# Storing converted weight units from ScalarE's queue, one step behind their conversion

## The chip, the cores and the metric

The kernel runs on one core of a Trainium2 chip. The metric is the device time of one execution in microseconds (us). The engines are named as the profile names them: PE (TensorE's matmuls) and PEld (its weight loads), DVE (VectorE), ACT (ScalarE), POOL (GpSimd) and SP (SyncE). SP computes nothing; it issues transfers.

## The reference

Three stages follow one another, all in float32.

1. A linear recurrence with a complex decay over 768 positions, for 2 x 8 heads of width 48: `S = a * S + k v^T`, `y = q S`. Its output is reshaped to `x` with 1536 rows of 384.
2. A mixture of 8 experts: each row goes to the expert with the largest of `x @ w_gate`, and becomes `gate_w * (relu(x @ w1[e]) @ w2[e])`, with `w1[e]` 384 x 1024 and `w2[e]` 1024 x 384.
3. A gated product: `out = ((x @ w_a) * (x @ w_b)) @ w_out`, with `w_a`, `w_b` 384 x 1536 and `w_out` 1536 x 384. These three arrive as 64-bit floating-point numbers, and the kernel itself turns them into 32-bit ones.

## The kernel before

The three stages run in this order; the change lies in the second, the expert stage, from about 235 to 380 us.

**The expert stage.** Each of the 8 experts is four steps `fp`, so there are 32 steps `i = 4 * e + fp`, written out in one loop (L1064). In a step, TensorE runs `hmm(i)` (18 products for 256 hidden columns, L1023, and ACT's and DVE's readout of them) and `ymm(i - 1)` (18 products of the second layer, L1039). A product in float32 is made of three: every operand is split into a high part (ACT) and a low part (DVE: value minus high part). So behind each `hmm` ACT writes `hh` (L1027) and DVE writes `hl` (L1028), and `ymm` reads both. In the step `fp = 1` TensorE also turns the rows of the next expert (`expert_x`, L1004), split by ACT and DVE into `XTT` (L1011, L1013). After the last `ymm` of an expert its sums are copied to `x2h` (ACT, L1042) and `x2l` (DVE, L1043). `bounds()` puts one tiny product `fp` (L986) into step 10.

**Weights of the next expert.** `wload(e + 1, 1)` at `fp = 0` and `wload(e + 2, 0)` at `fp = 2` load 1536 KB each on SP's queue (L717) into two buffers in turn; a load waits until the split of what the buffer held is done. `wsplit` splits a quarter of an expert's weights per step: ACT's cast (L730), then DVE's subtraction (L734).

**Units of the last stage's weights.** The first third of `w_a`, `w_b` and `w_out` is converted during the earlier stages, in 12 units of 384 KB (0 to 3 of `w_a`, 4 to 7 of `w_b`, 8 to 11 of `w_out`). A unit is loaded into a tile `raw` on SP's queue (`raw_load`, L746, L748), converted by five operations of DVE and one of ACT into a tile `cvt` (`conv_g`, L757 to L765), put on the list `pend`, and stored as 192 KB of float32 into a DRAM array `wf` (`store`, L774). Units 0 to 2 go this way in the first stage. The dictionary `UE` (L1047) says which unit is converted beside which expert: unit 3 beside expert 0, units 4 and 5 beside expert 1, 6 and 7 beside expert 2, then one per expert. Where there are two, the first is converted in step `fp = 2` and the second in `fp = 3`; where there is one, it takes both steps. `store()` is called at `fp = 0` of the next expert (L1089), on SP's queue, after that step's loads; for the last unit it is called at the start of step 28 (L1071).

`m2load(w)` reads `wf[w]` back in steps 26, 27 and 28 (L791), and `m2split` splits it (L795, L796): parts 0 and 1 in steps 28 and 29, part 2 after the last `ymm`.

**Buffers.** `hh`, `hl`, `raw`, `cvt` and the rows `R` of an expert are all tiles with the tag "T", for which there are nine buffers (L61, L62). A new tile takes over a buffer once all that reads or writes its last content is done; for a `cvt` tile that is its store.

**Order.** The order of the instructions of each engine is that of the program (L37, a manual schedule). Each engine takes its own instructions in order, and so does each queue of transfers: one that waits holds up those behind it on the same queue.

Of the kernel before, what the change touches and what calls it, by code (L numbers as in the profile page):

```python
# [35 lines left out]
def build(tc, *args, **kw):  # L36
    with tc.manual_schedule():  # L37
        body(tc, *args, **kw)


def body(tc, q, k, v, a_re, a_im, w_gate, w1, w2, cap, w_a, w_b, w_o, out, dbg=None):
    nc = tc.nc
# [9 lines left out]
    def tS(shape, dt, name):  # L52
        return mp.tile(shape, dt, tag="S", name=name, bufs=2)
# [7 lines left out]
    def tT(shape, dt, name):  # L61
        return mp.tile(shape, dt, tag="T", name=name, bufs=9)  # L62
# [325 lines left out]
    def run(g):  # L388
        for _ in g:
            pass  # L390
# [323 lines left out]
    def wload(e, w):  # L714
        WR[w, e] = tS([128, 2, 3 * FF // 2], F32, f"wr{w}_{e}")
        src = (w1, w2)[w][e]
        nc.sync.dma_start(WR[w, e].rearrange("p a r -> p (a r)").rearrange("p (k f) -> p k f", k=(KD, KF)[w]), src.rearrange("(k p) f -> p k f", p=128))  # L717

    def wsplit(e, part):
        run(wsplit_g(e, part, 1))  # L720
# [48 lines left out]
            return x.rearrange("p (k f) -> p k f", k=KD)[:, :, u * 128:(u + 1) * 128]  # L769
        return x[:, u * CU:(u + 1) * CU]  # L770

    def store():
        for dst, src in pend:
            nc.sync.dma_start(dst, src)  # L774
        pend.clear()

    def conv_out(w, u, t):
# [11 lines left out]
    def m2load(w):  # L789
        m2r[w] = tS([128, 1536], F32, f"m2r{w}")  # L790
        nc.sync.dma_start(m2r[w], wf[w])  # L791

    def m2split(w):
        hl, r = m2tile(w, 0), m2r[w]
        A.copy(hl[:, 0], r)  # L795
        V.tensor_tensor(hl[:, 1], r, hl[:, 0].bitcast(F32), ALU.subtract)  # L796
# [29 lines left out]
    for c in range(NC):  # L826
# [39 lines left out]
        if c < NU0:  # L866
            store()
            if c + 1 < NU0:
                conv_load(u0[c + 1][0], 0, u0[c + 1][1], cv[:, (c + 1) % 2, :2 * CU])
            x = cv[:, c % 2]  # L870
            conv_out(*u0[c], conv(u0[c][0], 0, u0[c][1], x[:, 2 * CU:3 * CU], x[:, 3 * CU:]))
        if c == 3:
            store()
            wload(0, 0)
            wload(0, 1)
# [4 lines left out]
    def raw_load(n):  # L880
        conv_load(u0[n][0], 0, u0[n][1], tT([128, 2 * CU], I32, f"raw{n}"))

    def conv_tt(n):
        x = tT([128, 2 * CU], I32, f"cvt{n}")
        yield from conv_g(u0[n][0], 0, u0[n][1], x[:, :CU], x[:, CU:])
        conv_out(*u0[n], x[:, CU:].bitcast(F32))
# [10 lines left out]
    def pse(shape, name, tag, bufs):  # L897
        return ep.tile(shape, F32, tag=tag, name=name, bufs=bufs)
# [96 lines left out]
    def load_x(e):  # L995
        R = Rt[e] = tT([SP, 2, DM], F32, f"R{e}")
        after(nc.sync.dma_start(R, xs[e * NT:e * NT + SLOT].rearrange("(a p) d -> p a d", p=SP)), xs_sc)

    def expert_x(e):
        R = Rt[e]  # L1000
        xp = [pse([128, KD, SP], f"xp{e}_{a}", f"xp{a}", 1) for a in range(2)]
        for a in range(2):
            for kk in range(KD):
                PE.transpose(xp[a][:, kk], R[:, a, kk * 128:(kk + 1) * 128], ident[:SP, :SP])  # L1004
        X = XT[e] = XTT[:, e % 2]

        def o(i):
            return X[:, i].rearrange("p k (a t) -> p k a t", a=2)

        for a in range(2):  # L1010
            A.copy(o(0)[:, :, a], xp[a])  # L1011
        for a in range(2):
            V.tensor_tensor(o(1)[:, :, a], xp[a], o(0)[:, :, a].bitcast(F32), ALU.subtract)  # L1013

    def hmm(e, fp):
        hp = pse([128, 2, SLOT], f"h{e}_{fp}", "h", 3)
        W = WHL[0, e]
        for f2 in range(2):
            f = fp * 2 + f2
            i = 0  # L1020
            for a, b in ((0, 0), (1, 0), (0, 1)):
                for kk in range(KD):
                    PE.matmul(hp[:, f2], W[:, a, kk, f * 128:(f + 1) * 128], XT[e][:, b, kk], start=(i == 0), stop=(i == 3 * KD - 1))  # L1023
                    i += 1
        hi = tT([128, 2, SLOT], F32R, f"hh{e}_{fp}")
        lo = tT([128, 2, SLOT], F32R, f"hl{e}_{fp}")
        A.activation(hi, hp, AF.Relu)  # L1027
        V.scalar_tensor_tensor(lo, hp, 0.0, hi.bitcast(F32), ALU.max, ALU.subtract)  # L1028
        Hp[e, fp] = hi, lo

    def ymm(e, fp):
        if fp == 0:
            yps[e] = [y[:, e % 2] for y in YPS]
        W = WHL[1, e]
        for d in range(KD):
            for f2 in range(2):
                f = fp * 2 + f2
                for i, (a, b) in enumerate(((0, 0), (0, 1), (1, 0))):
                    PE.matmul(yps[e][d], W[:, a, f, d * 128:(d + 1) * 128], Hp[e, fp][b][:, f2], start=(f == 0 and i == 0), stop=(f == KF - 1 and i == 2))  # L1039
            if fp == 3:  # L1040
                hi, lo = (x[:, ds(offs[e], SLOT)] for x in x2[d])
                A.copy(hi, yps[e][d])  # L1042
                V.tensor_tensor(lo, yps[e][d], hi.bitcast(F32), ALU.subtract)  # L1043
# [17 lines left out]
    def load_off(e):  # L1061
        offs[e] = nc.values_load(off_i[:, e:e + 1], engines=[mybir.EngineType.Activation, mybir.EngineType.DVE], min_val=0, max_val=NT, skip_runtime_bounds_check_because="exclusive prefix sums of counts that add up to NT")
    bd = bounds()
    for i, (e, fp) in enumerate(seq):  # L1064
        if fp == 0 and e + 1 < E:
            load_x(e + 1)
            wload(e + 1, 1)
        if fp == 2 and e + 2 < E:
            wload(e + 2, 0)
        if i == 28:  # L1070
            store()  # L1071
        if i >= 26 and i < 29:
            m2load(i - 26)
        hmm(e, fp)
        if i == 0:
            next(tb)
        if i == 6:
            run(tb)
        if fp == 2:
            load_off(e)  # L1080
        if i in (2, 4, 10, 11, 12):
            next(bd, None)
        if i > 0:
            ymm(*seq[i - 1])
        if fp == 1 and e + 1 < E:
            expert_x(e + 1)
        us = UE.get(e, ())
        if fp == 0 and us:
            store()  # L1089
        if fp < len(us) and e > 0:  # L1090
            raw_load(us[fp])
        if len(us) == 2 and fp > 1:
            run(conv_tt(us[fp - 2]))
        elif us and fp == 2:
            cg = conv_tt(us[0])
            next(cg)
            next(cg)
        elif us and fp == 3:
            run(cg)
        if e + 1 < E:  # L1100
            wsplit(e + 1, fp)
        elif fp < 2:
            m2split(fp)
# [257 lines left out]
```

## Time and profile before

| | us |
|---|---|
| three runs | 610.43, 617.68, 617.88 (median 617.68) |
| profiled execution | 616.19 |
| its span, first to last instruction | 614.5 |
| PE busy | 513.5 (84%) |
| DVE busy | 436.3 (71%) |
| ACT busy | 277.3 (45%) |
| mean granted clock of TensorE | 0.948 |

The busy shares are of the whole span. The granted clock is a share of full speed (2.4 GHz). An engine's idle time is listed with what ended it, the releaser.

### The profile page before, as it was taken

To read this page: it belongs to the slowest core of one execution; us is meant where nothing else is said; L and a number is where in the kernel's file an instruction comes from. 1 tells how busy PE (TensorE), PEld (TensorE's weight loads), DVE (VectorE), ACT (ScalarE), POOL (GpSimd) and SP (SyncE) were. 2 spreads that over 40 slices of the span, in tenths; PEclk is the share of its full clock that TensorE was granted. 3 is DMA by queue.
4 is the path that set the end of the run, shared out by engine and by line. 5 is a ranking of instruction groups with operands and counts; after the bars stand their busy time and mean duration, and the time that the engine had idled before them with its cause. 6 is when DMAs were issued, how large, how long until landed. Compare 5 with 4: busy or idle time off the path is not lost. (4 is left out here: it accounts for less than half of the span.)

```text
span 614.5 us, 10390 instructions
## 1 busy us (share of the span) xinstructions
PE 513.5 (84%) x4030; PEld 456.8 (74%) x4030; DVE 436.3 (71%) x957; ACT 277.3 (45%) x491; POOL 78.4 (13%) x127
## 2 busy tenths in 40 slices
PE   0064754799899878987999999999999999999993
PEld 0022322579889748987899999888888888888992
DVE  6899999974998964796687884766666767623331
ACT  6566563684344443643566563343443333211220
POOL 2000000040134273011221000000000000002121
PEclk9987687869999988998999999999999999999998
DMA  4248742298966127868587644121212121001010
GB/s 153 53 144 217 227 112 81 61 170 189 217 182 236 48 85 228 262 167 275 179 269 253 219 160 126 51 78 51 78 53 78 52 77 53 2 0 52 20 58 30
DMA packets 63249, 77.56 MB, mean 126 GB/s; under 512 B 29464, under 2 KB 53144, under 8 KB 63192
## 3 DMA queue, kind: packets, MB, share of 16 engines
q1 hardware_dynamic: 60208, 68.75, 38.6%
q0 software_dynamic: 2576, 7.68, 4.4%
q8 instruction: 33, 0.54, 0.4%
q10 hardware_dynamic: 408, 0.39, 0.2%
q14 instruction: 24, 0.20, 0.1%
HBM read 61.27 MB, written 15.54 MB: 125 GB/s over the span
## 5 line engine op out<-in xcount | busy, mean ns | idle before, releaser
L1126 PE MATMUL ab<-x2h,m2h 128*128 128x512 f32 (+1 forms) x480 | 142.1, 369 | 0.0
L1126 PEld LDWEIGHTS ab<-x2h,m2h 128*128 128x128 f32 x480 | 87.4, 188 | 14.4
L1126 PE MATMUL ab<-x2l,m2h 128*128 128x512 f32 (+1 forms) x240 | 88.8, 370 | 0.0
L319 PE MATMUL n<-temps,ident 128*128 128x384 f32 x40 | 28.0, 866 | 56.9 <-ACT temps L316 56.9
L1142 PE MATMUL o<-m2h,gh 128*128 128x384 f32 x288 | 73.6, 336 | 0.0
L1023 PE MATMUL h<-XTT,whl 128*128 128x240 f32 x576 | 71.8, 279 | 0.6 <-ACT XTT L1011 0.6
L1039 PE MATMUL yps<-hh,whl 128*128 128x240 f32 x384 | 71.7, 279 | 0.8 <-DVE x2l L1043 0.8
L1023 PEld LDWEIGHTS h<-XTT,whl 128*128 128x128 f32 x576 | 68.6, 193 | 0.9 <-ACT XTT L1011 0.9
L734 DVE TENSOR_TENSOR whl<-wr,whl 128x1536 fp32r<-128x1536 f32 (+1 forms) x38 | 57.1, 1502 | 12.8 <-ACT whl L730 12.7
L319 PEld LDWEIGHTS n<-temps,ident 128*128 128x128 f32 x40 | 12.0, 325 | 70.0 <-issue 37.2
L1039 PEld LDWEIGHTS yps<-hh,whl 128*128 128x128 f32 x384 | 61.7, 194 | 1.0 <-DVE x2l L1043 0.9
L1133 DVE TENSOR_TENSOR g<-ab,g 128x512 f32<-128x512 f32 (+1 forms) x40 | 25.5, 638 | 45.8 <-PE ab L1126 45.8
L1039 PE MATMUL yps<-hl,whl 128*128 128x240 f32 x192 | 53.9, 281 | 2.3 <-DVE hl L1028 2.3
L1142 PEld LDWEIGHTS o<-m2h,gh 128*128 128x128 f32 x288 | 52.5, 188 | 2.4
L1126 PEld LDWEIGHTS ab<-x2l,m2h 128*128 128x128 f32 x240 | 45.2, 188 | 6.9
L1142 PE MATMUL o<-m2h,gl 128*128 128x384 f32 x144 | 48.5, 337 | 0.0
L1134 ACT CAST gh<-g 128x512 fp32r<-128x512 f32 (+1 forms) x40 | 23.2, 580 | 56.1 <-DVE g L1133 52.7
L730 ACT CAST whl<-wr 128x1536 fp32r<-128x1536 f32 x32 | 47.4, 1480 | 0.0
L1135 DVE TENSOR_TENSOR gl<-g,gh 128x512 fp32r<-128x512 f32 (+1 forms) x40 | 25.6, 639 | 25.8 <-ACT gh L1134 25.3
L1160 POOL DMA_INDIRECT out_dram<-acc,MT x12 | 11.7, 974 | 251.0 <-DVE acc L1158 248.7
L1039 PEld LDWEIGHTS yps<-hl,whl 128*128 128x128 f32 x192 | 37.0, 193 | 2.7 <-DVE hl L1028 2.7
L1132 ACT COPY g<-ab 128x512 f32<-128x512 f32 (+1 forms) x40 | 21.6, 541 | 28.9 <-PE ab L1126 27.7
(233 smaller groups left out, 946.0 us busy)
## 6 DMA issues: line engine op xcount, KB each, us to landing
wr<-in_moe_w_dram SPq DMA_DIRECT2D x16, 1536.0 KB
kid<-KL SPq DMA_DIRECT2D x5, 896.0 KB
cv<-in_moe_w_a_dram SPq DMA_DIRECT2D x11, 384.0 KB
KN<-kid SPq DMA_DIRECT2D x5, 672.0 KB
cv<-in_moe_w_b_dram SPq DMA_DIRECT2D x8, 384.0 KB
cv<-in_moe_w_out_dram SPq DMA_DIRECT2D x8, 384.0 KB
xs<-zt POOLq DMA_DIRECT2D x1, 2880.0 KB, 17.9
R<-xs SPq DMA_DIRECT2D x8, 360.0 KB
```

The source lines that it names most:

```text
L319: PE.matmul(n2, ident, sq[:, :, c], start=(c == 0), stop=(c == 1))
L730: A.copy(hl[:, 0, sl], WR[w, e][:, hf])
L734: V.tensor_tensor(hl[:, 1, x], WR[w, e][:, hf, i * n:(i + 1) * n], hl[:, 0, x].bitcast(F32), ALU.subtract)
L1023: PE.matmul(hp[:, f2], W[:, a, kk, f * 128:(f + 1) * 128], XT[e][:, b, kk], start=(i == 0), stop=(i == 3 * KD - 1))
L1039: PE.matmul(yps[e][d], W[:, a, f, d * 128:(d + 1) * 128], Hp[e, fp][b][:, f2], start=(f == 0 and i == 0), stop=(f == KF - 1 and i == 2))
L1126: PE.matmul(p, W[:, a].rearrange("p (k f) -> p k f", k=KD)[:, kk, (f % 4) * 128:(f % 4 + 1) * 128], x2[kk][b][:, c0:c0 + n], start=(i == 0 ...
L1132: A.copy(g, ps[0])
L1133: V.tensor_tensor(g, ps[1], g, ALU.mult)
L1134: A.copy(gh, g)
L1135: V.tensor_tensor(gl, g, gh.bitcast(F32), ALU.subtract)
L1142: PE.matmul(ops[s4], g[a][:, s4 * 128:(s4 + 1) * 128], W[:, b, f % 4], start=(f % 4 == 0 and i == 0), stop=(f % 4 == 3 and i == 2))
L1160: d = G.indirect_dma_start(out=out, out_offset=bass.IndirectOffsetOnAxis(ap=MT[:, i, 0:1].bitcast(U32), axis=0), in_=acc, in_offset=None)
```

## The change

`store` gets the engine that issues it as an argument. In the expert stage it is called in every step, right behind `hmm` and so behind `hh` on ACT's queue, and the two calls on SP are taken out. `m2load(2)`, which reads what the store of unit 11 writes, moves behind the store in step 28. The calls of `store()` in the first stage stay on SP.

```diff
-    def store():
+    def store(eng=nc.sync):
         for dst, src in pend:
-            nc.sync.dma_start(dst, src)
+            eng.dma_start(dst, src)
         pend.clear()
...
-        if i == 28:
-            store()
-        if i >= 26 and i < 29:
+        if i >= 26 and i < 28:
             m2load(i - 26)
         hmm(e, fp)
+        store(nc.scalar)
+        if i == 28:
+            m2load(2)
...
         us = UE.get(e, ())
-        if fp == 0 and us:
-            store()
         if fp < len(us) and e > 0:
             raw_load(us[fp])
```

## Rows read from the trace of the kernel before

**Rows 1.** Busy us by engine (x instructions), then PEclk, DMA share, GB/s.
```profile
285.00:287.00 2.00, 2.00 (x11) 2.00 (x11) 2.00 (x3) 0.00 (x0) 1.11 (x1) 0.50 0.75 193
```

**Rows 2.** Waits from 235 to 385 us: engine, line, releaser, total us, times, longest.
```profile
DVE hl L1028 <- DMA wf<-cvt: 9.9, 2, 5.9
...
ACT hh L1027 <- DMA wf<-cvt: 5.0, 4, 1.8
...
PE fp L986 <- DVE XTT L1013: 4.4, 1, 4.4
...
PE yps L1039 <- DVE hl L1028: 2.3, 2, 1.5
...
PE yps L1039 <- DVE x2l L1043: 0.8, 1, 0.8
```

**Rows 3.** Timeline of PE: start us, us, instruction [idle before and releaser].
```profile
258.45 2.26 PE L1023 MATMUL h<-XTT,whl 128*128 128x240 f32 x18
...
262.58 2.18 PE L1023 MATMUL h<-XTT,whl 128*128 128x240 f32 x18
...
277.37 2.26 PE L1023 MATMUL h<-XTT,whl 128*128 128x240 f32 x18
284.01 0.19 PE L986 MATMUL fp<-ones_f,okm 128*1 128x1 f32 x2 [4.38 <-DVE XTT L1013]
...
287.88 2.18 PE L1023 MATMUL h<-XTT,whl 128*128 128x240 f32 x18
...
300.56 2.27 PE L1023 MATMUL h<-XTT,whl 128*128 128x240 f32 x18
...
306.44 2.19 PE L1023 MATMUL h<-XTT,whl 128*128 128x240 f32 x18
```

**Rows 4.** Timeline of DVE around the conversions of units 4 and 5.
```profile
266.88 0.56 DVE L765 SCALAR_TENSOR_TENSOR cvt<-raw,cvt 128x384 f32<-128x384 f32 x1
...
271.54 0.56 DVE L765 SCALAR_TENSOR_TENSOR cvt<-raw,cvt 128x384 f32<-128x384 f32 x1
...
273.68 0.65 DVE L1028 SCALAR_TENSOR_TENSOR hl<-h,hh 128x480 fp32r<-128x480 f32 x1
...
275.19 1.75 DVE L734 TENSOR_TENSOR whl<-wr,whl 128x1536 fp32r<-128x1536 f32 x1
282.86 0.66 DVE L1028 SCALAR_TENSOR_TENSOR hl<-h,hh 128x480 fp32r<-128x480 f32 x1 [5.92 <-DMA wf<-cvt]
```

**Rows 5.** Timeline of SP's queue: transfers as they are issued.
```profile
273.79 0.37 SPq L717 DMA_DIRECT2D wr<-in_moe_w_dram  x1
274.21 1.75 SPq L774 DMA_DIRECT2D wf<-cvt  x2
...
295.99 1.25 SPq L774 DMA_DIRECT2D wf<-cvt  x2
```

**Rows 6.** Timeline of ACT in steps 7 and 8.
```profile
267.23 0.59 ACT L1027 ACTIVATE hh<-h 128x480 fp32r<-128x480 f32 x1
270.01 0.58 ACT L760 ACTIVATE raw<-raw 128x384 f32<-128x384 f32 x1 [2.19 <-DVE cvt L757]
...
271.85 0.58 ACT L1027 ACTIVATE hh<-h 128x480 fp32r<-128x480 f32 x1
...
273.05 1.50 ACT L730 CAST whl<-wr 128x1536 fp32r<-128x1536 f32 x1
```

**Rows 7.** Issue of one transfer, ns min/median/max: on ACT's queue, the stores on SP's.
```profile
L416 ACTq DMA_DIRECT2D temps<-in_a_im_dram x3: 603/608/1213, 0.9 to 2.8; - x3
...
L774 SPq DMA_DIRECT2D wf<-cvt x9: 426/581/1617, 254.3 to 365.6; - x9
```

**Rows 8.** The last store, its reader, and ACT's split of what that loads.
```profile
365.64 0.43 SPq L774 DMA_DIRECT2D wf<-cvt  x1
370.34 0.32 SPq L791 DMA_DIRECT2D m2r<-wf  x1
...
379.51 1.48 ACT L795 CAST m2h<-m2r 128x1536 fp32r<-128x1536 f32 x1
```

## The prediction

> **What bounds the kernel now.** I first read the busy time of each engine in short stretches. In the expert stage TensorE is busy in nearly every microsecond, so only what TensorE itself waits for can be gained there. So the second view was the list of waits of this stage, from 235 to 385 us, read for TensorE alone: there are three matmul entries in all, 4.4, 2.3 and 0.8 us [rows 2]. Nothing else stops TensorE between 235 and 385 us.
>
> Next I asked what stands behind the 4.4. TensorE's program order is hmm(10), a tiny matmul `fp`, ymm(9), hmm(11). The timeline shows hmm(10) from 277.37 to 279.63 and then nothing until `fp` at 284.01 [rows 3]; `fp` needs a PSUM buffer that VectorE frees with its XTT subtraction, and VectorE does that right after the lo half of step 9, `hl`. VectorE finished its weight split at 276.94 and then stood still for 5.92 us until 282.86 [rows 4]. The releaser named is the transfer wf<-cvt. `hl` does not read wf or cvt. It writes a tile of tag "T", of which there are nine buffers, and the buffer it was given had held the converted unit 4. A buffer whose content is still being stored can't be overwritten. This is the mechanism on which everything else rests.
>
> Why is that store so late? The conversion of unit 4 ended at 266.88 + 0.56 = 267.44 [rows 4]. Its store left SP only at 274.21, in one piece of 1.75 us with unit 5's, right behind a 1536 KB weight load issued at 273.79 [rows 5], which itself waits for the weight split of step 7. So unit 4 lay ready for 6.8 us, and then its 192 KB queued behind 1536 KB: 282.86 - 274.21 = 8.65 us from issue to release.
>
> The same happens one expert later: units 6 and 7 leave at 295.99 [rows 5], step 13's `hl` waits 9.9 - 5.9 = 4.0 us for the transfer, and TensorE loses 1.5 us of the 2.3 [rows 2]. From expert 3 on there is one unit per expert. There it is ACT's `hh` that waits for the transfer, up to 1.8 us at a time [rows 2], and no TensorE entry answers to it: TensorE runs on.
>
> **The change part by part.** *Nine stores move from SP's queue to ACT's, behind hh of the next step.* For units 3, 5, 7, 8, 9, 10 and 11 that is the same step as before; only units 4 and 6 go one step earlier. But on SP a store also stood behind the load of the next expert's second weights; on ACT it does not.
>
> *Gain at the first place.* Unit 4: ACT's hh of step 7 ends at 267.23 + 0.59 = 267.82 [rows 6], the conversion is 0.4 us older, so the store is issued at 267.8 without waiting. Its landing is bounded from both sides by two stores of the trace: 4.7 us (unit 11, 365.64 until the load that waits for it at 370.34 [rows 8]) and 8.65 us. So it lands between 272.5 and 276.5, and VectorE could not start step 9's hl before 276.94 anyway. The stall goes entirely. What it costs now: from the start of hmm(10) to that of hmm(11) are 287.88 - 277.37 = 10.51 us; the same stretch one expert earlier, hmm(6) to hmm(7), took 262.58 - 258.45 = 4.13 [rows 3]. The difference, **6.38 us**, is more than the 4.4 us of waiting: after the idle time the granted clock is 0.50, the 1.2 GHz level [rows 1], and the matmuls of ymm(9) run at half speed. Without the idle time I count this back too.
>
> *Gain at the second place.* hmm(14) to hmm(15): 306.44 - 300.56 = 5.88 us, less 4.13: **1.75 us** [rows 3].
>
> *Gain in experts 3 to 6.* ACT's four waits for the transfer, 5.0 us together [rows 2], disappear; TensorE never waited for them, so 0.
>
> *What takes the stall's place.* VectorE is the next to be late: with two units per expert it is filled with conversions and splits, and its lag already shows as TensorE waits of 0.84 (in the 2.3) and 0.8 us in steps 7 and 8 [rows 2]. Those two lie before the removed stall and stay. With the 6 us of slip gone, steps 10 to 12 can show the same: VectorE works through unit 6, which must have been loaded in time behind the 1536 KB. Bounds: 0, and the two known lags together, 1.6 us. I take **0.4**, nearer 0, since steps 11 and 12, the other two with such a load, show no lag of this kind today, and raw loads no longer stand behind two stores.
>
> *Cost on ACT.* One DMA issue on ACT took 0.6 us (median of three); stores on SP took 0.43 to 1.62 us [rows 7]; below 0.43 there is nothing to gain. I take 0.6, since it is the only row of ACT. Behind the store of unit 4 ACT's next work starts at 270.01, 2.2 us later: hidden. Behind unit 5's store (hh of step 8 ends 272.43, conversion ends 272.10 [rows 4, 6], so no wait) stand three x2h copies, the weight cast and hh of step 9. The cast would end at 273.05 + 1.50 + 0.6 = 275.15, and VectorE takes it up at 275.19 [rows 4, 6]: just hidden. At 1.6 us VectorE would start 1 us later, and step 9's hl with it; ymm(9) needs hl only once TensorE has finished hmm(10), at 279.63, so that too is covered. In one-unit experts ACT has more room. Sum 0, up to 1 us.
>
> *Relief on SP.* SP loses nine issues of 0.6 us; loads behind them go out earlier by that. Nobody waits for SP's own time; 0.
>
> *The last load, m2load(2), moves behind the store of unit 11.* It reads what that store writes. The store left SP at 365.64, the load at 370.34, and its reader on ACT starts at 379.51, behind the last copies of the expert stage [rows 8]. On ACT the store goes out after hh of step 28, some 2 us earlier than on SP. Even if it were 4 us later the load (4.7 us) would land by 379.0. Cost 0.
>
> **Sum**, against the profiled execution's own 616.19 us (span 614.5 and 1.69 around it): 616.19 - 6.38 - 1.75 + 0.4 = 608.5. The profiled run lies 1.5 us under the median of the three runs shown (617.68; the lowest is 610.43), so the same sum on the median gives 609.9. I say **609**.
>
> **The rivals.** *(a) The queue makes no difference to the landing, and the buffer is asked for sooner.* The row: the store of unit 4 needed 8.65 us behind 1536 KB, and at 267.8 another weight load is still under way. The tile allocator hands buffers on in the order in which they come free; with the store a step earlier, unit 4's buffer may go to step 8's hl (273.68) rather than step 9's. If the store again takes 8.65 us, it lands at 276.5, and VectorE stands for 2.8 us in step 8 [rows 4], which has no slack (TensorE already waits there). At the second place I count the 1.75 us as lost again. The gain shrinks from 8.1 to 3.6: 612.6, on the median 614.1. For it: the transfer engines are shared, seen in the 8.65. Against: two things must come together. The Trainium skill, DMA: Bandwidth & Descriptors, section "Issuing engines are not separate DMA queues", speaks for it: transfers started by any engine run on the same 16 DMA engines, so issuing from another one saves only sequencer time. By that rule alone the queue gives nothing, and only the earlier issue counts. The same page, "Queues, rings and completion order", says that each DMA engine takes the queues it has work for in turn, packet by packet; by that a store on ACT's queue need not sit out the whole load. No row of the trace has both queues loaded at once.
>
> *(b) It doesn't do what it says.* The releaser at 282.86 is inferred. If what really landed then were the weight load that was in flight ahead of the store, the stall would stay: 616 to 618. Against: hl reads no loaded tile, and the same releaser stands at both places.
>
> *(c) Slower.* An issue on ACT blocks everything behind it. If each of the nine takes over 0.9 us out of TensorE's path, the 8.1 us are spent; at SP's longest 1.62 us each, none hidden, 9 x 1.6 = 14.6 against 8.1: 622.7. The place would be the three x2h copies behind each store at an expert's start. Against: ACT's own issues took 0.6 us [rows 7], and at the tightest place that is just hidden.
>
> *(d) More than the sum.* The three runs differ by 7 us. If the lowest, 610.43, still holds the two stalls, the changed kernel would show 603 to 604. More likely the low run is one in which the store happened to land early.
>
> **How the numbers follow.** Forecast 0.68, (a) 0.16, (b) 0.06, (c) 0.04, (d) 0.06. The likeliest case's own range is 606 to 611.5 (1.6 us of VectorE lag and 1 us of ACT above, no lag and the profiled base below). The range for 8 in 10 goes from 604.5 to 614.5, which takes in (a) and leaves out (b), (c) and most of (d). Two per cent, about what a measurement of this kernel can tell from no change, is 12.4 us: under 605.3 lie most of (d) and a tail of the forecast, 0.09; over 630 only a worse form of (c), 0.02; the rest, 0.89, is within 2%.
>
> **What would show it.** Right: no wait of hl for wf<-cvt; hmm(10) to hmm(11) about 4.2 us; no stretch of granted clock 0.50 after it; ACT issues of about 0.6 us at some 0.1 us after hh. Wrong: a wait of hl or hh for wf<-cvt in steps 8 or 12 (a); the wait at step 9 unchanged, now put down to a load (b); x2h or the weight cast late behind a store, with TensorE waiting for x2l (c); VectorE waiting for a raw load in step 10, by more than 1.6 us.

## The result, and the profile after

The changed kernel takes 608.36 us (median of four runs, 605.37 to 609.29) against 617.3 for the kernel before. The ratio is 0.987, with a 95% interval of 0.982 to 0.992. A second measurement, `again` below, gave 608.81 against 619.19, ratio 0.983 (0.979 to 0.987). The forecast was 609.

Four entries of the list of waits of the changed kernel, from 230 to 375 us (engine, line, releaser, total us, times, longest):

```profile
DVE hl L1028 <- ACT hh L1027: 7.0, 2, 3.9
...
PE yps L1039 <- DVE x2l L1043: 1.6, 2, 0.8
DVE cvt L757 <- DMA raw<-in_moe_w_b_dram: 1.4, 1, 1.4
...
PE yps L1039 <- DVE hl L1028: 0.8, 1, 0.8
```

In this list hl waits for ACT's hh alone; the entries of hl and of hh for wf<-cvt [rows 2] are gone, and so is the wait of `fp`, 4.4 us. Two entries are new in size: TensorE's wait for x2l has doubled, and VectorE waits for a raw load.

The timeline of PE in the changed kernel, to be read beside [rows 3] (hmm of steps 6, 7, 10, 11, 13, 14, 15):

```profile
254.11 2.26 PE L1023 MATMUL h<-XTT,whl 128*128 128x240 f32 x18
258.24 2.18 PE L1023 MATMUL h<-XTT,whl 128*128 128x240 f32 x18
...
273.00 2.26 PE L1023 MATMUL h<-XTT,whl 128*128 128x240 f32 x18
277.44 2.18 PE L1023 MATMUL h<-XTT,whl 128*128 128x240 f32 x18
...
285.71 2.19 PE L1023 MATMUL h<-XTT,whl 128*128 128x240 f32 x18
288.74 0.38 PE L1039 MATMUL yps<-hh,whl 128*128 128x240 f32 x1 [0.84 <-DVE x2l L1043]
291.41 2.26 PE L1023 MATMUL h<-XTT,whl 128*128 128x240 f32 x18
295.54 2.18 PE L1023 MATMUL h<-XTT,whl 128*128 128x240 f32 x18
```

Step 10 falls from 10.51 to 4.44 us and step 14 from 5.88 to 4.13. Step 13 grows from 4.60 to 5.70. The two-microsecond stretches show no slow clock behind step 10; the one with the end of the changed kernel's ymm(9) and the start of hmm(11) reads (columns as in [rows 1]):

```profile
276.00:278.00 2.00, 2.00 (x20) 2.00 (x19) 1.53 (x2) 0.00 (x0) 0.92 (x1) 1.00 1.09 365
```

where the clock column (third from the end) shows 1.00; in before it read 0.50 during ymm(9) [rows 1].

What VectorE and ACT do in steps 7 to 10 now. First ACT with its queue, then VectorE (beside [rows 4, 6]):

```profile
262.89 0.57 ACT L1027 ACTIVATE hh<-h 128x480 fp32r<-128x480 f32 x1
263.12 0.54 ACTq L774 DMA_DIRECT2D wf<-cvt  x1
265.64 0.57 ACT L760 ACTIVATE raw<-raw 128x384 f32<-128x384 f32 x1 [2.19 <-DVE cvt L757]
...
267.49 0.55 ACT L1027 ACTIVATE hh<-h 128x480 fp32r<-128x480 f32 x1
267.76 0.52 ACTq L774 DMA_DIRECT2D wf<-cvt  x1
268.39 0.89 ACT L1042 CAST x2h<-yps 128x240 f32 x3 [0.34 <-issue]
```

```profile
269.32 0.65 DVE L1028 SCALAR_TENSOR_TENSOR hl<-h,hh 128x480 fp32r<-128x480 f32 x1
...
270.83 1.74 DVE L734 TENSOR_TENSOR whl<-wr,whl 128x1536 fp32r<-128x1536 f32 x1
272.50 0.65 DVE L1028 SCALAR_TENSOR_TENSOR hl<-h,hh 128x480 fp32r<-128x480 f32 x1
...
278.90 0.36 DVE L757 TENSOR_SCALAR cvt<-raw 128x384 int32<-128x384 int32 x1 [1.38 <-DMA raw<-in_moe_w_b_dram]
```

The store of unit 4 leaves at 263.12, before hh has even ended (263.46): the issue does not wait for the computation in front of it on ACT. Its packets are the only ones of ACT's queue then. By queue (q1 is SP's, q10 ACT's; packets, MB, share of the 16 DMA engines), the first two lines for 264 to 266 us, the third for 266 to 268:

```profile
q1 hardware_dynamic: 219, 0.31, 61.3%
q10 hardware_dynamic: 378, 0.19, 40.2%
...
q10 hardware_dynamic: 22, 0.01, 1.6%
```

None moved before 264 us, and all had moved by 267: the store met only the end of the loads issued at 258.15 and 258.57, and took under 4 us. Steps 8 and 9's hl (269.32, 272.50) wait for no transfer. The last line of VectorE is the place where it is late now: it starts unit 6 with a wait of 1.38 us.

### The profile page after: what moved, and what is told of

Same layout as the page of the kernel before. It is cut to its first block, busy times and chain, and to the rows that moved or that the text cites. A ratio compares the mean times of both kernels' runs of the same rounds, so it can differ in the third digit from the quotient of the medians.

```text
span 603.7 us, 10385 instructions
## 1 busy us (share of the span) xinstructions
PE 508.1 (84%) x4030; PEld 452.2 (75%) x4030; DVE 435.4 (72%) x957; ACT 276.8 (46%) x491; POOL 79.6 (13%) x127
## 5 line engine op out<-in xcount | busy, mean ns | idle before, releaser
L319 PE MATMUL n<-temps,ident 128*128 128x384 f32 x40 | 26.7, 835 | 56.2 <-ACT temps L316 56.2
L1039 PE MATMUL yps<-hh,whl 128*128 128x240 f32 x384 | 70.2, 276 | 1.6 <-DVE x2l L1043 1.6
L1039 PEld LDWEIGHTS yps<-hh,whl 128*128 128x128 f32 x384 | 60.4, 190 | 2.0 <-DVE x2l L1043 2.0
```

The lines of the kernel that those rows point to most:

```text
L319: PE.matmul(n2, ident, sq[:, :, c], start=(c == 0), stop=(c == 1))
```

## The experiments

All profiles fit into one table. "Step 2" is the start of hmm(2); up to it the programs do the same work, and it scatters from 237 to 246 us. "Step 2 to end" runs from there to the end of the span. The last four columns are differences of such starts: steps 10 and 11 together, step 13, step 14, and steps 15 to 30 together.

| kernel | step 2 | step 2 to end | 10, 11 | 13 | 14 | 15-30 |
|---|---|---|---|---|---|---|
| before | 241.66 | 372.8 | 14.55 | 4.60 | 5.88 | 66.53 |
| before_again | 243.43 | 374.5 | 14.61 | 4.58 | 5.88 | 68.27 |
| before_third | 243.70 | 373.7 | 14.59 | 4.60 | 5.26 | 68.24 |
| changed | 237.31 | 366.4 | 8.48 | 5.70 | 4.13 | 66.53 |
| again | 241.19 | 365.8 | 8.48 | 5.69 | 4.13 | 66.52 |
| after_third | 241.65 | 365.5 | 8.47 | 4.91 | 4.13 | 66.54 |
| sp_new_place | 238.98 | 368.4 | 8.48 | 6.86 | 4.12 | 67.43 |
| sp_ahead_of_load | 244.06 | 365.1 | 8.48 | 4.71 | 4.13 | 66.54 |
| act_old_place | 242.12 | 366.0 | 8.48 | 5.11 | 4.14 | 67.14 |
| act_behind_load | 245.99 | 365.5 | 8.48 | 5.11 | 4.14 | 66.71 |
| act_two_behind | 242.20 | 370.3 | 9.09 | 5.78 | 4.13 | 68.84 |
| no_store_4_to_7 | 242.58 | 365.7 | 8.48 | 5.65 | 4.14 | 66.51 |
| raw_first | 242.55 | 366.6 | 8.48 | 6.41 | 4.14 | 66.52 |
| four_pieces | 239.54 | 369.6 | 8.47 | 6.85 | 4.13 | 66.89 |

**How large is the gain?** `again` and `after_third` are the changed kernel unedited, `before_again` and `before_third` the kernel before.

> The changed kernel once more, to size the gain: its profile beside the one of before loses 6.6 us between step 3 and step 15 of the expert stage, and 4.3 us ahead of step 3, where the two programs are alike. If only the former is the change, the ratio comes out near 0.989 (610 against 617); if the latter is part of it, near 0.982.

> The kernel before, a third profile, to size the gain. From step 2 to the end: 372.8 and 374.5 us in its first two, 366.4 and 365.8 in the two of the changed kernel. If the timed difference (9 to 10 us) is all in the expert stage, this is over 375; if part of it is chance in the first stage, it is 373 to 374.5 again and the start of step 2 lies anywhere from 237 to 246 us.

> The kernel before, unchanged, for a second profile. In the five profiles without the stall the stretch from step 3 to step 15 of the expert stage takes 54 to 55 us, in the one of before 60.66. The timed medians differ by 9 to 10 us, though. If the stall is larger in a usual execution of before than in the one profiled, this profile shows more than 10.5 us between hmm(10) and hmm(11), or a third stalled step; if the rest is chance of the first stage, it shows 60.7 again.

> The changed kernel, a third profile: step 2 to the end 365.8 to 366.4 again, the start of step 2 anywhere from 237 to 246 us.

`again` came out at 0.983, which spoke for a larger gain than the first pair of traces shows. The next two profiles of before show where part of it is: steps 15 to 30 take 68.3 and 68.2 us there, not 66.5. In the trace of before_again, hh waits for the store of unit 8, and this time TensorE feels it (the waits from 230 to 400 us, then rows of ACT, DVE and PE):

```profile
ACT hh L1027 <- DMA wf<-cvt: 9.4, 4, 2.9
DVE hl L1028 <- DMA wf<-cvt: 9.2, 2, 5.2
```

```profile
325.62 0.57 ACT L1027 ACTIVATE hh<-h 128x480 fp32r<-128x480 f32 x1 [2.55 <-DMA wf<-cvt]
326.23 0.66 DVE L1028 SCALAR_TENSOR_TENSOR hl<-h,hh 128x480 fp32r<-128x480 f32 x1 [1.36 <-ACT hh L1027]
...
331.58 0.38 PE L1039 MATMUL yps<-hl,whl 128*128 128x240 f32 x1 [0.21 <-DVE hl L1028]
```

TensorE's named waits in steps 15 to 30 of that trace, 0.21 and 0.34 us, are less than the 1.7 us that these steps are longer. The steps that grow are 20, 23, 24 and 28, each time behind such a wait of hh; what the rest of their growth is made of is not shown.

From step 2 to the end the three profiles of before average 373.7 us and the three of the changed kernel 365.9: 7.8 us. The timed medians differ by 8.9 and 10.4. The rest, 1.1 to 2.6 us, would have to lie ahead of step 2, where before starts at 241.7 to 243.7 and all other kernels at 237.3 to 246.0 (mean 241.7). That is scatter as far as these profiles can tell; whether a microsecond of it is more stays open.

**Is it the store?** Units 4 to 7 are not stored at all; `wf[0]` is read back in place of the part of `w_b` that they make up.

```diff
-        conv_out(*u0[n], x[:, CU:].bitcast(F32))
+        if n not in (4, 5, 6, 7):
+            conv_out(*u0[n], x[:, CU:].bitcast(F32))
...
-        nc.sync.dma_start(m2r[w], wf[w])
+        nc.sync.dma_start(m2r[w], wf[w if w != 1 else 0])
```

> The kernel before without the stores of units 4 to 7 at all (the part of w_b they make up is left out, and part 0 is read back in its place). If the waits of steps 9 and 13 are for those stores, they vanish with no other edit: gain as in the changed kernel, 6 to 7 us. If the releaser was named wrongly and hl really waited for the weight load, the 10.5 us between hmm(10) and hmm(11) stay.

610.06 us, ratio 0.987 (0.983 to 0.991). Steps 10, 11 and 14 are those of the changed kernel. Here unit 4's buffer goes to the rows of expert 3, so hl of step 9 also has another buffer than in before. That the wait was for the store is seen in the built program of before itself: hl of step 9 waits for a semaphore (a count that one instruction raises and another waits for) whose count the store of unit 4 completes, and hl of step 13 for one that the store of unit 6 completes. So the waits were for these stores, and having no stores is no better than having them early (610.06 against 608.81 us).

**The queue, or the place in it?** Three edits move the store without the other half of the change, and a fourth puts it behind the load on the other queue.

```diff
 sp_new_place (from the changed kernel)
-        store(nc.scalar)
+        store()
```

> The changed kernel with the stores still on SP's queue: behind hh of every step, as in the change, but issued by SP. If what counts is that the store of unit 4 leaves one step earlier, ahead of the 1536 KB load and not behind it, step 9's hl doesn't wait and most of the gain stays (5 to 6.6 us); units 5 and 7 still stand behind that load on SP, so something may wait up to 1.5 us for unit 5. If what counts is the other queue, hl waits as before and the time is that of before (616 to 618).

```diff
 sp_ahead_of_load (from before)
             load_x(e + 1)
+            if i > 0:
+                store()
             wload(e + 1, 1)
...
-        if fp == 0 and us:
-            store()
```

> The kernel before with the stores still on SP's queue and still at the next expert, but put ahead of that step's 1536 KB load instead of behind it. If the place in SP's queue was the whole cost, unit 4 lands before anything asks for its buffer and the 10.5 us between hmm(10) and hmm(11) fall to 4.4. Here hh of step 9 takes the buffer of unit 5, which leaves at the same moment; with 3 to 5 us to land it may wait 1 to 3 us. Time 609 to 613. If a transfer of 192 KB needs 8 us whatever is ahead of it, the stall only moves to step 9 and the time is that of before.

```diff
 act_old_place (from before; the same at both calls)
-            store()
+            store(nc.scalar)
```

> The kernel before with its stores issued by ACT, at the old places (behind the ymm of the next expert's first step, so behind the three x2h copies on ACT). Unit 4's store then leaves at about 273.2 of before's clock and not at 274.2, beside the 1536 KB load and not behind it on one queue. If the queue frees it from that load, it lands in about 4.7 us, at 278, and step 9's hl waits 1 us: gain 5 us. If the engines are shared so that the queue gives nothing, it lands after 8.6 us, at 282, hl waits 5 us, and the gain is under 1.5 us.

```diff
 act_behind_load (from act_old_place)
-        if fp == 0 and us:
-            store(nc.scalar)
...
             wsplit(e + 1, fp)
+            if fp == 0 and us:
+                store(nc.scalar)
```

> The stores on ACT's queue, but at the end of the next expert's first step, behind ACT's weight cast: unit 4's store then leaves some 0.5 us after the 1536 KB load has left on SP's queue, where in before it left 0.4 us after it on the same queue. If a second queue really gets its turn beside the load, the store lands in about 5 us and step 9's hl waits 1.5 to 2.5 us (gain 3.5 to 5). If all transfers drain in the order of their issue, it lands after 8.6 us as before, hl waits 5 to 6 us, and the time is that of before.

```diff
 act_two_behind (from the changed kernel)
-        store(nc.scalar)
+        if fp == 1 or i == 28:
+            store(nc.scalar)
```

> The changed kernel with its stores on ACT's queue one step later (in the second step of the next expert; unit 11 as in the change). Unit 4 and 5 then leave about 1 us after the 1536 KB load has left on SP's queue. The packets of each queue in short stretches show what a second queue gives: if the two take turns, ACT's 2 x 192 KB pass within about 3 us of their issue while SP's load is still moving, and nothing waits for them (time of the changed kernel, 608 to 610). If they drain in the order of their issue, ACT's packets come only after the load's, 7 us later, and hh of step 10, which here takes unit 4's buffer, waits some 2 us.

Both SP versions lose the stall: sp_new_place 609.89 us, 0.986 (0.981 to 0.991), sp_ahead_of_load 609.1 us, 0.986 (0.980 to 0.993). In sp_ahead_of_load (SP's queue):

```profile
269.86 5.20 SPq L774 DMA_DIRECT2D wf<-cvt  x2
276.22 0.38 SPq L717 DMA_DIRECT2D wr<-in_moe_w_dram  x1
```

Unit 4 leaves SP at 269.86, soon after its conversion ends (269.84), and 6.4 us ahead of the load; in before it left 0.4 us behind it [rows 5]. The expected wait of hh for unit 5 did not come: its store left only when its conversion had ended, about 274.5, and was through when hh of step 9 started at 277.11, 2.6 us later. This version does without ACT and has the shortest time from step 2 to the end, 365.1 us. Its buffers are dealt anew as well: unit 4's goes to raw of unit 6, unit 5's to hh of step 9. So the two SP versions show that another place in SP's queue is enough; how much of it is the earlier leaving and how much the other tile that takes the buffer is not separated in them, since no run moves the store and leaves its buffer to hl of step 9.

sp_new_place pays in another place, step 13:

```profile
293.71 0.84 PE L1004 MATMUL xp<-ident,R 120*128 120x120 f32 x6 [0.94 <-DMA R<-xs]
```

The rows of expert 4 get the buffer of unit 6. Its store left at 283.15, 3 us behind a weight load on SP's queue, and SP issued the load of these rows only at 289.88, with the next weight load behind it. Steps 15 to 30 are longer too; there hh waits for stores again.

act_old_place (610.19 us, 0.987, 0.983 to 0.990) and act_behind_load (607.9 us, 0.983, 0.979 to 0.987) tell less than planned. In act_old_place unit 4's store left at 272.39, 1.8 us ahead of the load (274.20). In act_behind_load it left at 276.27 and the load only at 278.08; it never stood behind the load. ACT issued it ahead of the three x2h copies and the cast (277.33) that precede it in the program:

```profile
276.27 0.55 ACTq L774 DMA_DIRECT2D wf<-cvt  x1
276.60 0.60 ACT L1042 CAST x2h<-yps 128x240 f32 x2
...
277.08 0.37 ACT L1042 CAST x2h<-yps 128x240 f32 x1
```

In both, the built program gives unit 4's buffer to hh of step 10, not to hl of step 9, so nothing asked for it early.

act_two_behind did what act_behind_load was meant to do (SP's queue, then ACT's with hh of step 10):

```profile
275.19 0.37 SPq L717 DMA_DIRECT2D wr<-in_moe_w_dram  x1
```

```profile
275.47 0.61 ACTq L774 DMA_DIRECT2D wf<-cvt  x1
...
283.55 0.57 ACT L1027 ACTIVATE hh<-h 128x480 fp32r<-128x480 f32 x1 [2.62 <-DMA wf<-cvt]
```

The store left 0.3 us behind the load, on its own queue, and still took 8.1 us, as against 8.65 behind the load on one queue. The packets by queue show it. The first line is from 279 to 280 us, the next two from 280 to 281, the last two from 282 to 283:

```profile
q1 hardware_dynamic: 245, 0.38, 103.9%
...
q1 hardware_dynamic: 207, 0.32, 84.1%
q10 hardware_dynamic: 135, 0.07, 22.8%
...
q1 hardware_dynamic: 225, 0.23, 67.2%
q10 hardware_dynamic: 224, 0.11, 37.2%
```

Until 280 us no packet of ACT's queue moved; from then on the two queues shared. Its time, 613.71 us, 0.993 (0.989 to 0.997), gives about half of the gain back. From step 2 to the end it takes 370.3 us, as against 365.9 and 373.7.

**What is left in step 13?** The raw load goes out first in its step.

```diff
+        us = UE.get(e, ())
+        if fp < len(us) and e > 0:
+            raw_load(us[fp])
         if fp == 0 and e + 1 < E:
             load_x(e + 1)
             wload(e + 1, 1)
...
-        us = UE.get(e, ())
-        if fp < len(us) and e > 0:
-            raw_load(us[fp])
```

> The changed kernel with the raw load of the step issued at the step's start, ahead of the 1536 KB load (and the rows of x) instead of behind it. What is left over in the changed kernel is 1.1 us in step 13, which I put down to VectorE: it waits 1.4 us for unit 6's raw load in step 10 and is late from there on. If so, the wait goes, hmm(13) to hmm(14) falls from 5.7 to about 4.6, and the time by 1 us. If VectorE is late by its own work alone, the wait goes and the 5.7 stay. If SP then waits for a buffer of raw in front of the weight load, the weight casts come late and it is slower.

611.15 us, 0.988 (0.984 to 0.992): no gain. The edit also changes who gets which buffer: unit 6's goes to hh of step 12, which asks for it sooner (ACT, then PE):

```profile
292.74 0.57 ACT L1027 ACTIVATE hh<-h 128x480 fp32r<-128x480 f32 x1 [2.98 <-DMA wf<-cvt]
```

```profile
294.43 0.38 PE L1039 MATMUL yps<-hh,whl 128*128 128x240 f32 x1 [1.56 <-DVE x2l L1043]
```

The wait for the raw load itself is gone, as expected: VectorE starts unit 6 (second line) right behind hl of step 10. The wait for hh stands in its place (third line, hl of step 12):

```profile
282.04 0.65 DVE L1028 SCALAR_TENSOR_TENSOR hl<-h,hh 128x480 fp32r<-128x480 f32 x1
282.60 0.51 DVE L757 TENSOR_SCALAR cvt<-raw 128x384 int32<-128x384 int32 x1
...
293.35 0.66 DVE L1028 SCALAR_TENSOR_TENSOR hl<-h,hh 128x480 fp32r<-128x480 f32 x1 [1.77 <-ACT hh L1027]
```

So the time does not answer the question, but the traces together do. Steps 12 and 13 take 8.64 us in before; beside what they take more stands how long VectorE waited in steps 10 to 12, for unit 6's raw load where nothing else is said:

| kernel | VectorE's wait | steps 12 and 13 above 8.64 |
|---|---|---|
| sp_ahead_of_load | 0.20 | 0.11 |
| after_third | 0.37 | 0.32 |
| act_old_place | 0.61 | 0.51 |
| act_behind_load | 0.62 | 0.52 |
| again | 1.13 | 1.10 |
| changed | 1.38 | 1.29 |
| no_store_4_to_7 | 0.66, and 0.46 put down to ACT | 1.05 |
| raw_first | 1.77, for hh | 1.82 |

The growth is the wait to within about 0.1 us. What is left in step 13 is VectorE's lateness with unit 6, and in the changed kernel the raw load sets it. That a raw load in time would give this back is argued from the table; no run shows it without another wait in its place.

**Is ACT's issue hidden?** Each store in four pieces.

```diff
-            eng.dma_start(dst, src)
+            if eng is nc.sync:
+                eng.dma_start(dst, src)
+            else:
+                for x in range(0, 128, 32):
+                    eng.dma_start(dst[x:x + 32], src[x:x + 32])
```

> The changed kernel with each of its nine stores issued on ACT in four pieces of 32 partitions: 36 issues and not 9, some 1.6 us more of ACT per store. If ACT's issues are hidden, as the sum has it, the time stays within 1 us of the changed kernel's. If they lie on the path (the slower rival), each store costs the 1.6 us: 9 x 1.6 = 14 us, 622.

612.53 us, 0.991 (0.987 to 0.995): 3.7 us above the changed kernel's 608.81, between the two expectations. For units 3 to 7 four issues took 2.5 to 3.6 us, and TensorE feels them at the start of experts 1, 2 and 3, where the x2h copies stand behind them (ACT's queue, then PE, around step 12):

```profile
289.41 3.54 ACTq L778 DMA_DIRECT2D wf<-cvt  x4
```

```profile
293.91 0.38 PE L1043 MATMUL yps<-hh,whl 128*128 128x240 f32 x1 [2.00 <-DVE x2l L1047]
```

In the one-unit experts the same four issues cost 0.4 us in all (66.89 for steps 15 to 30). So four issues per store are not hidden where ACT has least room. That one issue is hidden rests on sp_ahead_of_load, which has none on ACT in this stage and is only 0.4 to 1.3 us shorter from step 2 to the end; steps 12 and 13 alone differ by 0.2 to 1.2.

## Why the prediction was right

*The mechanism* was right: hl waited for a buffer whose content was still being stored, since the store stood in SP's queue behind the weight load. The built program and no_store_4_to_7 show the cause, sp_ahead_of_load that another place in SP's queue is enough to remove the stall. In the changed kernel unit 4's buffer is asked for one step sooner than in before (hl of step 8, 269.32) and yet nothing waits, so there the earlier leaving does it. In none of the variants does hl of step 9 keep that buffer, so what the new deal of the buffers adds in them stays open.

*First place, 6.38 us*: measured 6.07 in steps 10 and 11 (14.55 to 8.48). The idle time and the slow clock behind it went together, as counted. 0.31 us of step 10 stays in every variant, and more in act_two_behind. Step 6, the yardstick, holds no product `fp`.

*Second place, 1.75 us*: measured 1.75, and 1.13 against the third profile of before.

*Experts 3 to 6, 0*: right for the profiled execution, whose steps 15 to 30 take 66.53 us before and after, and wrong for the two others of before, 1.7 us each. "TensorE never waited for them, so 0" was read from one execution, in which the waits ended just in time: 5.0 us of ACT's waiting in that profile, 9.4 in the next.

*What takes the stall's place, 0.4 us*: this term was mis-sized. Steps 12 and 13 grew by 1.3, 1.1 and 0.3 us in the three profiles, and with the 0.3 of step 10 the term is 1.6, 1.4 and 0.6. The place is the forecast one, VectorE with unit 6, and the upper bound was 1.6. The reason for leaning to 0 ("raw loads no longer stand behind two stores") did not hold: the raw load stands behind the 1536 KB in any case, and VectorE now asks for it sooner (its start of unit 6 waits 1.38 us).

*ACT, 0*: right as far as the traces tell; the issues took 0.33 to 0.60 us. They do not stand 0.1 us behind hh, as the prediction said: the first began while hh was still running. *m2load(2), 0*: right. Its reader starts at 368.61 in the changed kernel and waits for nothing.

*The landing*: the prediction's lower bound, 4.7 us, was too high. Unit 4's store was through in under 4 us in the changed kernel, and unit 5's within 2.6 us in sp_ahead_of_load. Nothing in the sum hung on it.

*Rival (a)* had the program right, and still did not happen. The built program does give unit 4's buffer to hl of step 8, one step sooner. It was also close on the second queue: 8.1 us behind the load on ACT's queue in act_two_behind, 8.65 on one queue. The Trainium skill's rule from DMA: Bandwidth & Descriptors, "Issuing engines are not separate DMA queues", agrees with these two numbers. The other rule quoted, from "Queues, rings and completion order", that each DMA engine takes the queues in turn, is seen there only from 280 us on: for the first 4.5 us after the issue no packet of the store moved beside the load. What saved the change is where its stores fall between the loads: unit 4's left at 263.12, 6.3 us ahead of the load at 269.43. It met only the end of the loads before it, where (a) had counted a whole one.

*The sum* said 7.73 us. From step 2 to the end it is 7.8 as the mean of three profiles of each: the two wrong terms, 0.8 us more in the stall's place and 1.15 us more in experts 3 to 6 (both as means of three), nearly cancel. That is luck. And the timed gain, 8.9 and 10.4 us, is 1.2 to 2.7 us more than the sum, which stays open: 7.73 off the 617.3 of before would have been 609.6, not 608.36. (b) fell with the built program and no_store_4_to_7, (c) with the 608.8 of the change and the 612.5 of four times as many issues. (d) did not come: of the eleven runs of the changed kernel the lowest is 604.80.

## What to carry to other kernels

When an engine waits for a transfer that it doesn't read, look for the buffer: what was in it, what still reads that, and what stands ahead of that reader in its queue. Here a 192 KB store behind a 1536 KB load in one queue took 8.65 us, and 8.1 behind it on a second queue. Ahead of the load it was out of the way on either queue. So see first whether the store can leave before the load; another queue helps to that end when its own queue is held up. Read a stall that is "just hidden" from more than one execution before it is put down as 0.

## What the runs showed that was not expected

ACT's queue runs ahead of ACT's computation: in the changed kernel the store is issued at 263.12 while hh runs until 263.46, and in act_behind_load at 276.27, ahead of three x2h copies and a cast (277.33) that precede it in the program. So in these two traces the place in the program did not fix when a transfer left relative to ACT's own computation.

A small edit in the program order changes which tile gets which of the nine buffers: unit 4's went to hl of step 9 (before), hl of step 8 (changed), hh of step 10 (act_old_place), raw of unit 6 (sp_ahead_of_load) or the rows of expert 3 (no_store_4_to_7). Several of the experiments were blunted by that.
